# Block 0 of a fused attention and two-MLP kernel: low parts issued before squares, weight conversions issued behind later landmarks

## The chip, the cores and the metric

The kernel runs on one core of a Trainium2 chip. The metric is the device time of one execution in microseconds (us), lower is better. Five engines run at the same time, each working through its own queue in order: PE (matrix multiply), DVE, ACT and POOL (vector work of different kinds), and SP, which here only issues DMA transfers.

## The reference

Attention over 4 batches, 8 heads, 576 positions and 64 channels per head. Four heads see a window of 32 positions back, four see every 32nd position. Its output, 2304 tokens of 512 channels, goes through a gated MLP with a root mean square norm and then through a second MLP without a nonlinearity:

```python
x = attention(q, k, v).transpose(0, 2, 1, 3).reshape(2304, 512)
xn = x / sqrt(mean(x * x) + 1e-6) * rms_g
g = xn @ w_gate;  val = xn @ w_val            # 512 -> 1536
x = (g * sigmoid(g) * val) @ w_out            # 1536 -> 512
out = ((x @ w_a) * (x @ w_b)) @ w_out2        # 512 -> 1536 -> 512
```

All of it is float32. Every large product is made of three matmuls on numbers split into a high part (rounded) and a low part (the rest): high by high, high by low, low by high.

## The kernel before

The 576 positions are cut into six blocks t = 0 to 5 of 96 positions in 4 batches, so 384 tokens each. In block t the loop over fc = 0 to 11 takes 128 of the 1536 hidden channels at a time (a chunk). For each chunk PE makes `g_ps` and `v_ps` (12 matmuls each, lines 478 to 480), DVE scales g by the inverse root (`sg`, line 750), ACT applies Silu (751), DVE multiplies (`h`, 761), ACT rounds h to its high part and POOL or DVE subtracts for the low part (502, 503), and PE adds the chunk into `y` (12 matmuls, the same lines). While block t runs its MLP, the attention of block t + 1 is made in slots between the chunks. Three PSUM tiles serve all `g_ps` and `v_ps`, so `v_ps` of chunk 1 waits for `sg` of chunk 0, and `g_ps` of chunk 2 waits for `h` of chunk 0. The second MLP follows after block 5.

Block 0 has two things more. Its attention has nothing to hide behind: local heads (`qk`, `smask`, `lmax`, `lexp`, `lnorm`, then `pt`, a transpose on PE of the softmax weights, `ptc`, its copy on ACT, and `pv`, the product with v) and strided heads (`sqk`, `sexp`, `snorm`, `spv`). The result is split into `xx` by `xhl`: ACT writes the high part (`xhi`, 384), DVE the low part (`xlo`, 386), and ACT squares (`sq`, 429) for a matmul with ones (433), whose root (`sqrt`, 445) gives `rinv` (447). And block 0 converts the weights of the first MLP, which arrive as 64 bit words, once for all blocks: per 128 x 512 third ACT scales the upper word (134), the lower word is shifted into `cz` (139 on ACT or 136 on DVE, by the table `LOW`), DVE joins both (142), ACT rounds to the high part (147), POOL subtracts (148). `gv` of chunks 1 to 10 is done two thirds at a time (128 x 1024), `wo`, the third for `y`, alone.

The engines' orders are not written by hand. The framework's scheduler lists each engine's instructions by their place in the program and by its own idea of times; `tc.issue_after(i)` (in `gate` and `behind`) puts the instructions of the block behind i in the queue if both are on the same engine, and adds no wait across engines. `GATES` names for each chunk which steps of the attention its conversion stands behind. Two readers of one PSUM tile on different engines are kept apart by the framework: the second one in the program waits for the first.

Of the kernel before, what the change touches and what calls it, by code (L numbers as in the profile page):

```python
# [10 lines left out]
F32 = mybir.dt.float32  # L11
# [4 lines left out]
ALU = mybir.AluOpType  # L16
# [9 lines left out]
NFC = FF // 128  # L26
# [15 lines left out]
          "ptc2 pv0 pvc0 pv1 pvc1 xst0 xst1 xstc0 id36 xstc1 rms rinv")  # L42
WARM = 20

GATES = ["pvm snorm sqr",
         "norm pvm snorm sqr",
         "pvr snorm xhi",
         "snorm sqr sqrt xhi",
         "rec sexp snorm sqrt xhi"]

# [14 lines left out]
WLO = ["PPP", "PPP", "PPP", "PPP", "PPP", "PPP",  # L65
       "PPP", "PPP", "PPP", "PPP", "PPP", "PPD"]

LOW = ["AAA"] * NFC
NEG = -1000000000.0
BIG = 3.0e38  # L70
SCALE = 1.0 / 8.0
# [3 lines left out]
def fused_kernel(ctx: ExitStack, tc: tile.TileContext, qtl, ktl, vl, qs, ks, vs, cst, w1, w2, out):  # L75
# [5 lines left out]
    nc = tc.nc  # L81

    def engine(c):
        return {"P": nc.gpsimd, "D": nc.vector}[c]
# [82 lines left out]
    def run(steps):  # L167
        for f in steps:
            f()
# [14 lines left out]
    def attention(t, pool, psum, banks):  # L184
# [4 lines left out]
        st = {}  # L189
        steps = {}  # L190

        def bank():
            return psum.tile([128, 512], F32, tag=next(banks), name="att")

        def piece(tag, name, bufs):
            return pool.tile([128, NTB], F32, tag=tag, name=name, bufs=bufs)
# [161 lines left out]
        def ptc(g):  # L358
            def f():
                rows, n, keys, units = GROUPS[g]  # L360
                k0 = 0 if g < 2 else 64
                src = st["pps", g][k0:k0 + n].rearrange("k (u h r) -> k u h r", h=2, r=rows // 2)
                for hf in range(2) if g == 2 else [g]:
                    dst = pts[hf][k0:k0 + n, :, :, k0:k0 + rows // 2]
                    nc.scalar.copy(dst, src[:, 4 * hf:4 * hf + 4] if g == 2 else src)
            return f

        def pv(p):
# [11 lines left out]
        def xhl(i, src):  # L380

            xx = act.tile([128, 2, NTB], F32R, tag="x", name="xx", bufs=8)
            hi, lo = xx[:, 0], xx[:, 1]
            st["xhi"] = nc.scalar.activation(hi, src, AF.Copy, scale=g_sb[:, i:i + 1])
            sq(i)()
            st["xlo"] = nc.vector.scalar_tensor_tensor(lo, src, g_sb[:, i:i + 1], hi.bitcast(F32), op0=ALU.mult, op1=ALU.subtract)
            xt[t, i] = xx

        def xsplit(i, src):
# [35 lines left out]
        def sq(i):  # L425
            def f():
                q_t = st["sq", i] = piece("sq", "sq", 2)
                src = st["ops" if i < 2 else "xps", i % 2][:, :NTB]
                nc.scalar.activation(q_t, src, AF.Square)
                if t == 0:  # L430
                    if i == 0:
                        st["rps"] = bank()
                    nc.tensor.matmul(st["rps"][:, :NTB], ones, q_t, start=i == 0, stop=i == 3)
                elif i:
                    engine(SQA[t]).tensor_tensor(q_t, q_t, st["sq", i - 1], op=ALU.add)
            return f
# [50 lines left out]
    def tmp(name):  # L487
        return act.tile([128, NTB], F32, tag="t", name=name, bufs=NTMP)

    made = []  # L490

    @contextmanager
    def behind(instructions):

        with ExitStack() as e:
            for i in instructions:
                e.enter_context(tc.issue_after(i))
            yield
# [17 lines left out]
    g_sb = cst_sb[:, 384:388]  # L516
# [19 lines left out]
    def load_late(which):  # L536
        raw.update(zip(which, load_pair(w1, which, pool)))

    def convert1(fc):
        t = gv[fc] = gv_slot(F32R, "gv")  # L540
        two = [raw.pop((fc, k)) for k in range(2)]
        if fc in FUSEDW:
            both, ready = gvraw[fc], t.rearrange("p k a n -> p (k a) n")
            run(conversion(both.rearrange("p k a n -> p (k a) n"), ready, pool, engine(WLO[fc][0]), LOW[fc][0]))
        else:
            run(zipped(*(conversion(two[k], t[:, k], pool, engine(WLO[fc][k]), LOW[fc][k]) for k in range(2))))

# [29 lines left out]
    @contextmanager  # L577
    def gate(fc):

        with ExitStack() as e:  # L580
            for key in GATES[min(fc, len(GATES) - 1)].split():
                e.enter_context(tc.issue_after(s0["st"][key].ins))
            yield
# [136 lines left out]
    for t in range(NB):  # L720
        if t == 1:
            apool.close()
            pool = apool.enter_context(tc.tile_pool(name="attn", bufs=1))
        if t == NB - 1:
            apool.close()
            cpool.close()
            pool = p2.enter_context(tc.tile_pool(name="forms", bufs=1, reuse_waits="tile"))
            early = [f for k in (4, 5, 0, 1, 2, 3) for f in convert_forms(k, k < 4)]
        nxt = attention(t + 1, pool, psum, itertools.cycle(["att"])) if t + 1 < NB else None
        x = [xt[t, cc] for cc in range(NCC)]  # L730
        for fc in range(NFC):
            if t > 0 and fc == 0:
                load_wo(t, 0)
            g_ps = psum.tile([128, 512], F32, tag="gv", name="g_ps", bufs=3)
            mm_in(g_ps[:, :NTB], gv[fc], 0, x)
            v_ps = psum.tile([128, 512], F32, tag="gv", name="v_ps", bufs=3)
            mm_in(v_ps[:, :NTB], gv[fc], 1, x)
            if t == 0 and fc + 1 < NFC:
                with gate(fc + 1):
                    convert1(fc + 1)  # L740
                if fc + 2 == NFC:
                    load_late([(NFC - 2, 2), (NFC - 1, 2)])
            if t == NB - 1:
                slab[fc] = wgt.tile([128, 4 * DM], F32 if fc in (0, 1, 11) else F32R, tag="gv", name="slab", bufs=NFC)
                with behind(made):
                    run(early[len(early) * fc // NFC:len(early) * (fc + 1) // NFC])
                    for k in [k for k in x0 if k <= fc]:
                        run(x0.pop(k))
            sg = tmp("sg")
            nc.vector.tensor_tensor(sg, g_ps[:, :NTB], ri[t], op=ALU.mult)  # L750
            nc.scalar.activation(sg, sg, AF.Silu)  # L751
            if fc == 1 and t > 0:
                evac_y(t - 1)
            if nxt is not None:
                attention_slot(nxt, fc)
            if prev is not None:
                emit_y(*prev)
            if t > 0 and fc + 1 < NFC:
                load_wo(t, fc + 1)
            h = tmp("h")  # L760
            made[:] = [nc.vector.tensor_tensor(h, sg, v_ps[:, :NTB], op=ALU.mult).ins]  # L761
            hl[t, fc] = split(h, engine(HLO0[fc] if t == 0 else HLO[t]))
            if t == 0:
                wt = wo[0, fc] = wo_tile()
                with gate(fc + 1):
                    run(conversion(raw.pop((fc, 2)), wt, pool, engine(WLO[fc][2]), LOW[fc][2], True))
                nc.sync.dma_start(wod[fc], wt.rearrange("p a n -> p (a n)").bitcast(F32))
                if fc % 2:
                    load_units(1)
                if fc == NFC - 3:  # L770
                    load_late([(NFC - 1, 0), (NFC - 1, 1)])
            prev = (t, fc)
    emit_y(*prev)
    evac_y(NB - 1)
# [238 lines left out]
```

## Time and profile before

| what | value |
|---|---|
| median of 3 runs | 980.23 us (980.2 to 981.69) |
| the profiled execution | 981.02 us |
| its span in the trace | 979.2 us |
| granted TensorE clock, mean | 0.986 |
| PE busy | 949.2 us |
| ACT, POOL, DVE busy | 427.7, 555.1, 620.4 us |

The span runs from the first to the last instruction of the program in the trace. All times in the trace's rows count from the span's start.

### The profile page before, as it was taken

The page shows a single profiled execution, that of the slowest core. Times are in us where ns is not written, and L with a number is a line of the kernel's source. Part 1 is how long each engine was busy: PE and PEld are TensorE (multiplying, and loading weights), DVE is VectorE, ACT ScalarE, POOL GpSimd, SP SyncE. Part 2 cuts the span into 40 slices and gives each one's busy share as a digit, 9 for nine tenths or more (in the row PEclk, how much of TensorE's full clock was granted, in tenths as well). Part 3 has the DMA queues.
Part 4 walks back from the last instruction along what each step waited for, and adds up shares of the span by engine and source line. Part 5 has one row for each costly group of instructions (what it writes and reads, how often), then busy time and mean ns, then how long its engine had stood idle before and what let it go on. Part 6 is the DMA issues. An engine that isn't in the chain of part 4 may idle for free.

```text
span 979.2 us, 14353 instructions
## 1 busy us (share of the span) xinstructions
PE 949.2 (97%) x5438; PEld 900.8 (92%) x5438; DVE 620.4 (63%) x891; ACT 427.7 (44%) x800; POOL 555.1 (57%) x418
## 2 busy tenths in 40 slices
PE   6899999999999999999999899999999999999998
PEld 5799989999999999999999899999999999999996
DVE  5568757638917984988565458667655655465534
ACT  4999645243534423433456455535434423122110
POOL 3489946558739776969468644754743424123211
PEclk7899999999999999999999999999999999999999
DMA  9963375435633643532687975897893973853701
GB/s 339 408 238 119 117 284 206 147 111 178 191 110 126 208 161 107 175 121 80 217 328 278 374 284 209 330 419 312 325 386 122 351 305 117 295 233 150 269 11 65
DMA packets 57364, 215.57 MB, mean 220 GB/s; under 512 B 5968, under 2 KB 14544, under 8 KB 51664
## 3 DMA queue, kind: packets, MB, share of 16 engines
q1 hardware_dynamic: 57296, 214.66, 59.7%
q8 instruction: 43, 0.70, 0.3%
q14 instruction: 25, 0.20, 0.1%
HBM read 172.17 MB, written 42.47 MB: 219 GB/s over the span
## 4 chain that ended last, share of the span: by engine, by line
PE 75%; DVE 6%; DMA 5%; POOL 5%; ACT 4%; issue 3%; SPq 1%; DVEq 0%; POOLq 0%; ACTq 0%
PE o L892 5%; PE o L894 5%; PE o L893 5%; PE Y L838 4%; PE Y L837 4%; PE Y L836 4%; PE y L478 3%; PE g_ps L478 3%; PE v_ps L478 3%; PE g_ps L480 3%; PE v_ps L480 3%; PE g_ps L479 3%; PE v_ps L479 3%; PE y L479 3%; PE y L480 3%
## 5 line engine op out<-in xcount | busy, mean ns | idle before, releaser
L148 POOL TENSOR_TENSOR hl<-c,hl 128x384 fp32r<-128x384 f32 x72 | 77.9, 1082 | 180.5 <-ACT hl L147 173.9
L245 POOL TENSOR_TENSOR prod<-kv_t,qs_t 128x512 f32<-128x512 f32 (+12 forms) x57 | 106.1, 1883 | 18.3 <-DMA kv_t<-in_ks 6.3
L503 POOL TENSOR_TENSOR hl<-h,hl 128x384 fp32r<-128x384 f32 x70 | 77.9, 1113 | 59.7 <-ACT hl L502 59.7
L478 PE MATMUL g_ps<-xx,gv 128*128 128x384 f32 x288 | 98.4, 342 | 5.1 <-DVE h L761 5.0
L478 PE MATMUL v_ps<-xx,gv 128*128 128x384 f32 x288 | 97.5, 339 | 3.5 <-DVE sg L750 3.0
L278 POOL TENSOR_TENSOR prod<-kv_t,S_t 128x512 f32<-128x512 f32 (+12 forms) x57 | 86.0, 1522 | 24.0 <-DVE S_t L270 7.7
L479 PE MATMUL y<-hl,wo 128*128 128x384 f32 x288 | 96.8, 341 | 1.3 <-POOL hl L503 1.3
L479 PE MATMUL v_ps<-xx,gv 128*128 128x384 f32 x288 | 97.8, 340 | 0.0
L480 PE MATMUL g_ps<-xx,gv 128*128 128x384 f32 x288 | 97.5, 339 | 0.0
L479 PE MATMUL g_ps<-xx,gv 128*128 128x384 f32 x288 | 97.3, 339 | 0.0
L480 PE MATMUL v_ps<-xx,gv 128*128 128x384 f32 x288 | 97.2, 338 | 0.0
L843 DVE TENSOR_TENSOR c<-c,Y 128x384 f32<-128x384 f32 x108 | 58.8, 551 | 58.6 <-PE Y L838 53.5
L480 PE MATMUL y<-hl,wo 128*128 128x384 f32 x288 | 95.4, 339 | 0.0
L281 DVE TENSOR_REDUCE xs_t<-prod 128x64 f32<-128x448 f32 (+17 forms) x57 | 85.2, 1515 | 6.0 <-POOL prod L278 5.8
L478 PE MATMUL y<-hl,wo 128*128 128x384 f32 x288 | 83.8, 343 | 2.8 <-DMA wo<-wod 1.8
L892 PE MATMUL o<-slab,hl 128*128 128x512 f32 x216 | 84.7, 393 | 1.0 <-DVE slab L901 0.5
L893 PE MATMUL o<-slab,hl 128*128 128x512 f32 x216 | 84.5, 392 | 0.0
L894 PE MATMUL o<-slab,hl 128*128 128x512 f32 x216 | 83.2, 394 | 0.0
L147 ACT CAST hl<-c 128x384 fp32r<-128x384 f32 x72 | 37.0, 514 | 94.2 <-DVE c L873 93.9
L751 ACT ACTIVATE sg<-sg 128x384 f32<-128x384 f32 x72 | 37.8, 525 | 87.6 <-DVE sg L750 78.0
L838 PE MATMUL Y<-slab,form 128*128 128x384 f32 x216 | 73.0, 338 | 0.0
L837 PE MATMUL Y<-slab,form 128*128 128x384 f32 x216 | 72.9, 338 | 0.0
(135 smaller groups left out, 2521.3 us busy)
## 6 DMA issues: line engine op xcount, KB each, us to landing
form<-formd SPq DMA_DIRECT2D x32, 1792.0 KB, 10.5
wo<-wod SPq DMA_DIRECT2D x60, 512.0 KB, 3.3
raw<-in_w SPq DMA_DIRECT2D x42, 512.0 KB, 7.4
gv_raw<-in_w SPq DMA_DIRECT2D x30, 512.0 KB, 10.0
formd<-form SPq DMA_DIRECT2D x6, 1792.0 KB, 7.0
formd<-forms SPq DMA_DIRECT2D x6, 1792.0 KB, 12.9
slab<-x2d SPq DMA_DIRECT2D x24, 384.0 KB, 4.5
wod<-wo SPq DMA_DIRECT2D x12, 512.0 KB, 3.4
```

The lines of the kernel that those rows point to most:

```text
L148: lo_eng.tensor_tensor(lo, x, hi.bitcast(F32), op=ALU.subtract)
L245: nc.gpsimd.tensor_tensor(pr, st["ks", g][:, :, :n, :], st["qs"][:, heads(g), mm:mm + 1, :].to_broadcast([128, G, n, D]), op=ALU.mult)
L278: st["pvm"] = nc.gpsimd.tensor_tensor(pr, st["vs", g][:, :, :n, :], st["S"][:, heads(g), mm, :n, None].to_broadcast([128, G, n, D]), op=AL ...
L281: st["pvr"] = nc.vector.tensor_reduce(st["xs"][:, mm, heads(g), :], pr.rearrange("p g n d -> p g d n"), axis=X, op=ALU.add)
L478: nc.tensor.matmul(out_ps, w_hi, x_hi, start=start, stop=False)
L479: nc.tensor.matmul(out_ps, w_hi, x_lo, start=False, stop=False)
L480: nc.tensor.matmul(out_ps, w_lo, x_hi, start=False, stop=stop)
L837: nc.tensor.matmul(bank(n), hi, x[p][:, 1, c], start=False, stop=False, skip_group_check=not begins)
L838: nc.tensor.matmul(bank(n), lo, x[p][:, 0, c], start=False, stop=c == 1, skip_group_check=not begins)
L892: nc.tensor.matmul(o, h[:, 0, cols], w[0], start=n == 0, stop=False)
L893: nc.tensor.matmul(o, h[:, 0, cols], w[1], start=False, stop=False)
L894: nc.tensor.matmul(o, h[:, 1, cols], w[0], start=False, stop=n == len(chunks) - 1)
```

## The change

Four edits, all for block 0: (1) in `xhl` the low part stands ahead of the square in the program; (2) `GATES` for chunks 0 and 1 add the copies of the transposed local weights (`ptc1`, `ptc2`), and chunk 2 now stands behind `sqr`, `sqrt` and `xhi`; `wo` of chunk 0 takes the gate of chunk 2; (3) the lower words of `gv` 1 and 2 are shifted on DVE instead of ACT; (4) the conversions of `gv` of chunk fc + 1 and of `wo` of chunk fc stand behind the three instructions that make `h` and its parts of chunk fc - 3.

```diff
-GATES = ["pvm snorm sqr",
-         "norm pvm snorm sqr",
-         "pvr snorm xhi",
+GATES = ["pvm snorm sqr ptc1",
+         "norm pvm snorm sqr ptc2",
+         "snorm sqr sqrt xhi",
          "snorm sqr sqrt xhi",
          "rec sexp snorm sqrt xhi"]
...
-LOW = ["AAA"] * NFC
+LOW = ["AAA", "DDA", "DDA"] + ["AAA"] * 9
...
-                    nc.scalar.copy(dst, src[:, 4 * hf:4 * hf + 4] if g == 2 else src)
+                    st[f"ptc{g}"] = nc.scalar.copy(dst, src[:, 4 * hf:4 * hf + 4] if g == 2 else src)
...
             st["xhi"] = nc.scalar.activation(hi, src, AF.Copy, scale=g_sb[:, i:i + 1])
+            st["xlo"] = nc.vector.scalar_tensor_tensor(lo, src, g_sb[:, i:i + 1], hi.bitcast(F32), op0=ALU.mult, op1=ALU.subtract)
             sq(i)()
-            st["xlo"] = nc.vector.scalar_tensor_tensor(lo, src, g_sb[:, i:i + 1], hi.bitcast(F32), op0=ALU.mult, op1=ALU.subtract)
...
+    h_made = {}
...
-                with gate(fc + 1):
+                with gate(fc + 1), behind(h_made.get(fc - 3, [])):
                     convert1(fc + 1)
...
-                with gate(fc + 1):
+                with gate(max(fc + 1, 2)), behind(h_made.get(fc - 3, [])):
                     run(conversion(raw.pop((fc, 2)), wt, pool, engine(WLO[fc][2]), LOW[fc][2], True))
...
+            if t == 0:
+                h_made[fc] = list(made)
```

On PE, ACT, DVE, POOL and SP the order changes from the first softmax to about the third chunk of block 1; behind that it is the same. Three places follow. The lines of the changed kernel are one higher from line 490 on, and one lower for `xlo` (385).

DVE from the sum of the last local softmax group (341, 343, 344, 345 normalise it) to the inverse root; `prod` is the product of the strided heads, `xx` the split result. Before:

```order
L341 TENSOR_REDUCE lsm<-s_t 64x8
L270 TENSOR_TENSOR S_t<-S_t,srs 128x12x3
L142 SCALAR_TENSOR_TENSOR cz<-gv_raw,cz 128x512
L343 TENSOR_SCALAR lsm<-lsm 64x8
L142 SCALAR_TENSOR_TENSOR cz<-gv_raw,cz 128x512
L344 RECIPROCAL lrs<-lsm 64x8
L281 TENSOR_REDUCE xs_t<-prod 128x256
L345 TENSOR_TENSOR s_t<-s_t,lrs 64x512
...
L386 SCALAR_TENSOR_TENSOR xx<-att,cst_sb,xx 128x384 x2
L142 SCALAR_TENSOR_TENSOR cz<-gv_raw,cz 128x1024
L142 SCALAR_TENSOR_TENSOR cz<-gv_raw,cz 128x512
L386 SCALAR_TENSOR_TENSOR xx<-att,cst_sb,xx 128x384 x2
```

And of the change:

```order
L341 TENSOR_REDUCE lsm<-s_t 64x8
L269 RECIPROCAL srs<-ssm 128x12
L343 TENSOR_SCALAR lsm<-lsm 64x8
L270 TENSOR_TENSOR S_t<-S_t,srs 128x12x3
L344 RECIPROCAL lrs<-lsm 64x8
L345 TENSOR_TENSOR s_t<-s_t,lrs 64x512
...
L136 TENSOR_SCALAR cz<-gv_raw 128x1024
L142 SCALAR_TENSOR_TENSOR cz<-gv_raw,cz 128x1024
L385 SCALAR_TENSOR_TENSOR xx<-att,cst_sb,xx 128x384
L136 TENSOR_SCALAR cz<-gv_raw 128x1024
L385 SCALAR_TENSOR_TENSOR xx<-att,cst_sb,xx 128x384 x3
```

Two joins (142) and a reduce no longer stand ahead of the normalisation 345, and two joins no longer stand ahead of the last two low parts; two shifts (136) are new.

ACT from the root of block 0 (445) to the first Silu (the activation into `sg`). Before:

```order
L445 ACTIVATE rms_t<-att,eps_sb 128x384
L134 ACTIVATE gv_raw<-gv_raw 128x1024
L139 ACTIVATE cz<-gv_raw 128x1024
L134 ACTIVATE gv_raw<-gv_raw 128x512
L134 ACTIVATE gv_raw<-gv_raw 128x1024
L139 ACTIVATE cz<-gv_raw 128x1024
L134 ACTIVATE gv_raw<-gv_raw 128x512 x2
L139 ACTIVATE cz<-gv_raw 128x512
L134 ACTIVATE gv_raw<-gv_raw 128x512
L134 ACTIVATE gv_raw<-gv_raw 128x1024
L147 CAST gv<-cz 128x2x512
L751 ACT_TABLE_LOAD
```

And of the change:

```order
L445 ACTIVATE rms_t<-att,eps_sb 128x384
L134 ACTIVATE gv_raw<-gv_raw 128x512
L139 ACTIVATE cz<-gv_raw 128x512
L134 ACTIVATE gv_raw<-gv_raw 128x1024
L134 ACTIVATE gv_raw<-gv_raw 128x512
L134 ACTIVATE gv_raw<-gv_raw 128x1024
L139 ACTIVATE cz<-gv_raw 128x1024
L134 ACTIVATE gv_raw<-gv_raw 128x512
L147 CAST wo<-cz 128x512
L147 CAST gv<-cz 128x2x512
L752 ACT_TABLE_LOAD
```

Eleven instructions stood between root and Silu's table, nine stand there now, other ones: behind the root there is now the whole conversion of `gv` 2 and of `wo` 0, which used to be done ahead of it.

DVE at the change from block 0 to block 1, where `S_t` are the strided scores of block 2 (their `prod` comes from POOL), `ys` is the output of block 0, `sg` and `h` belong to chunks of block 1. Before:

```order
L761 TENSOR_TENSOR h<-sg,v_ps 128x384
L248 TENSOR_REDUCE S_t<-prod 128x7
L248 TENSOR_REDUCE S_t<-prod 128x8
L750 TENSOR_TENSOR sg<-g_ps,rinv 128x384
L604 TENSOR_TENSOR ys<-y_537,rinv 128x384
...
L248 TENSOR_REDUCE S_t<-prod 128x9
L311 SCALAR_TENSOR_TENSOR s_t<-att,cst_sb 128x384
L248 TENSOR_REDUCE S_t<-prod 128x7
L320 TENSOR_REDUCE lmx<-s_t 128x4
L761 TENSOR_TENSOR h<-sg,v_ps 128x384
```

And of the change:

```order
L762 TENSOR_TENSOR h<-sg,v_ps 128x384
L751 TENSOR_TENSOR sg<-g_ps,rinv 128x384
L248 TENSOR_REDUCE S_t<-prod 128x7
L605 TENSOR_TENSOR ys<-y_537,rinv 128x384
...
L248 TENSOR_REDUCE S_t<-prod 128x9
L762 TENSOR_TENSOR h<-sg,v_ps 128x384
L311 SCALAR_TENSOR_TENSOR s_t<-att,cst_sb 128x384
```

The `sg` of block 1's second chunk now stands ahead of the reduces that wait for POOL, and its `h` ahead of the mask (311), one reduce and the maximum (320).

## Rows read from the trace of the kernel before

**Rows 1.** The page's head: span; busy time, share and instructions by engine.

```profile
span 979.2 us, 14353 instructions
PE 949.2 (97%) x5438; PEld 900.8 (92%) x5438; DVE 620.4 (63%) x891; ACT 427.7 (44%) x800; POOL 555.1 (57%) x418
```

**Rows 2.** Busy us (x instructions) of PE, PEld, DVE, ACT, POOL; granted clock, DMA, GB/s.

```profile
75.00:100.00 25.00, 23.95 (x162) 22.92 (x162) 22.20 (x26) 23.36 (x45) 25.00 (x14) 1.00 0.34 117
100.00:125.00 25.00, 24.34 (x147) 22.36 (x146) 17.57 (x21) 16.34 (x32) 22.15 (x17) 1.00 0.40 146
...
200.00:225.00 25.00, 25.00 (x149) 24.67 (x148) 12.75 (x18) 10.06 (x17) 14.85 (x12) 1.00 0.30 95
```

**Rows 3.** Timeline, 18 to 39 us: start, duration, engine, line, operation, tiles.

```profile
18.96 0.68 DVE L341 TENSOR_REDUCE lsm<-s_t 64x8 f32<-64x512 f32 x1 [0.86 <-ACT s_t L330]
...
22.70 0.67 DVE L345 TENSOR_TENSOR s_t<-s_t,lrs 64x512 f32<-64x512 f32 x1
...
25.93 0.64 ACT L365 COPY pt<-att 64x256 f32<-64x256 f32 x2
...
26.40 2.83 PE L375 MATMUL att<-pt,v_t 128*64 128x96 f32 x32
...
32.00 0.62 DVE L386 SCALAR_TENSOR_TENSOR xx<-att,cst_sb,xx 128x384 fp32r<-128x384 f32 x1 [1.45 <-ACT sq L429]
...
35.00 1.82 DVE L142 SCALAR_TENSOR_TENSOR cz<-gv_raw,cz 128x1024 uint32<-128x1024 uint32 x2 [2.38 <-ACT cz L139]
...
35.21 0.42 PE L478 MATMUL g_ps<-xx,gv 128*128 128x384 f32 x1
...
36.75 1.14 DVE L386 SCALAR_TENSOR_TENSOR xx<-att,cst_sb,xx 128x384 fp32r<-128x384 f32 x2
...
37.72 1.45 PE L433 MATMUL att<-sq,ones 128*128 128x384 f32 x4
```

**Rows 4.** Timeline of ACT and DVE, 39 to 51 us.

```profile
39.21 0.58 ACT L445 ACTIVATE rms_t<-att,eps_sb 128x384 f32<-128x384 f32 x1 [0.90 <-PE att L433]
39.69 1.16 ACT L134 ACTIVATE gv_raw<-gv_raw 128x1024 f32<-128x1024 f32 x1
39.83 2.55 DVE L447 RECIPROCAL rinv<-rms_t 128x384 f32<-128x384 f32 x1 [1.95 <-ACT rms_t L445]
...
40.71 1.15 ACT L139 ACTIVATE cz<-gv_raw 128x1024 uint32<-128x1024 uint16 x1
...
48.61 1.28 ACT L751 ACT_TABLE_LOAD   x1
49.90 0.52 ACT L751 ACTIVATE sg<-sg 128x384 f32<-128x384 f32 x1
```

**Rows 5.** ACT groups by form, 14 to 60 us: count, busy us, mean ns.

```profile
L134 ACT ACTIVATE gv_raw<-gv_raw 128x512 f32<-128x512 f32 x10 | 6.5, 677 | 0.0
```

**Rows 6.** Timeline of PE at its longest wait in block 0.

```profile
51.07 0.69 PE L478 MATMUL g_ps<-xx,gv 128*128 128x384 f32 x1 [4.71 <-DVE h L761]
```

**Rows 7.** Windows with a lower granted clock; columns as in rows 2.

```profile
50.60:53.90 3.30, 2.83 (x9) 2.83 (x10) 0.88 (x2) 3.30 (x5) 2.87 (x3) 0.50 1.07 405
...
153.00:156.30 3.30, 3.30 (x12) 3.30 (x11) 2.08 (x5) 3.27 (x11) 2.52 (x4) 0.50 0.37 103
```

**Rows 8.** DVE groups by form, 14 to 60 us.

```profile
L142 DVE SCALAR_TENSOR_TENSOR cz<-gv_raw,cz 128x1024 uint32<-128x1024 uint32 x6 | 7.3, 1215 | 5.8 <-ACT cz L139 5.8
```

**Rows 9.** POOL groups by form, 20 to 130 us; behind the bar idle us, releasers.

```profile
L148 POOL TENSOR_TENSOR gv<-cz,gv 128x1024 fp32r<-128x1024 f32 x10 | 26.8, 2685 | 14.5 <-ACT gv L147 12.2 <-DMA gv_raw<-in_w 2.3
```

**Rows 10.** Timeline, end of block 0.

```profile
116.77 0.69 ACT L134 ACTIVATE raw<-raw 128x512 f32<-128x512 f32 x1 [2.10 <-DMA raw<-in_w]
...
144.36 0.44 PE L478 MATMUL v_ps<-xx,gv 128*128 128x384 f32 x1 [1.04 <-DVE sg L750]
...
151.73 0.54 DVE L761 TENSOR_TENSOR h<-sg,v_ps 128x384 f32<-128x384 f32 x1
...
152.32 0.44 PE L478 MATMUL g_ps<-xx,gv 128*128 128x384 f32 x1 [0.31 <-DVE h L761]
```

## Prediction

> **What bounds the kernel now.** The page's head comes first: PE is busy for 949.2 of 979.2 us [rows 1], so all else counts only where PE waits. The table by stretches of 25 us, read next, says where that is. From 200 us on PE is busy without a gap at full clock, with DVE, ACT and POOL at 41 to 60% [rows 2]: a microsecond gained or lost before that moves the end by as much. Between 75 and 125 us PE is nearly full as well, but so are its suppliers: ACT 23.36 of 25 us, POOL 25.00 of 25, then 16.34 and 22.15 [rows 2]. What is left is the time to 51 us and the step from block 0 to block 1.
>
> The timeline of the front, read as a chain: the last softmax group is summed on DVE at 18.96 but normalised only at 22.70, because joins of weights that wait for ACT stand between. So the copies of its transpose come at 25.93, the product with v at 26.40, and the first real matmul, `g_ps`, at 35.21 [rows 3]. The first low parts wait for squares (1.45 us on ACT), the last two for joins, and end at 37.89, after `g_ps` has begun; the squares' matmuls come late too, and the root starts at 39.21 [rows 3, 4]. Then ACT works through eleven conversion instructions before it loads Silu's table at 48.61; the first Silu starts at 49.90 [rows 4]. `h` of chunk 0 needs it, `g_ps` of chunk 2 needs the PSUM tile that `h` frees, and PE waits 4.71 us for it, until 51.07 [rows 6]. Behind that wait the granted clock is 0.50, the lower of the two levels, 1.2 GHz, for 3.3 us [rows 7].
>
> **The change, part by part.** I start all chains from rows that the new order leaves in place and go on in the new order.
>
> *Softmax to first matmul.* The sum 341 ends at 19.64 as before. Now 269, 343, 270 and 344 follow, small operations of some 0.2 us, and 345 starts at about 20.5 and ends at 21.2 instead of 23.37: 2.2 us earlier. Before, its end stood 2.56 us ahead of the copies (25.93); with the same distance they start at 23.75. ACT has the second copy and four scalings and shifts of 128 x 512 ahead of them, from 20.3 on, 0.57 and 4 times 0.55, ready at 23.1, so it does not hold them. A 512 column step on ACT is 0.55 because 128 x 1024 steps are 1.02 from start to start for a duration of 1.15 [rows 4], and 0.68 [rows 5] less the same 0.13 is 0.55. The product with v, its 2.83 us and the warming matmuls up to `g_ps` are the same instructions as before (only the squares' matmuls move among them), so `g_ps` starts 2.2 earlier, at 33.0.
>
> *Low parts.* Their new place costs nothing and is worth little by itself: on DVE they end at about 31.8 instead of 37.89, so that all twelve matmuls of `g_ps` run in one piece. The two shifts on DVE are not in the trace. The nearest row is the join of 128 x 1024, 1.22 [rows 8], with two inputs where the shift has one; the lower end is half of it, 0.6, the upper 1.82, what two joins took together at 35.00 [rows 3]. I take 1.1, near the one join. With 1.82 twice the last low part would end at 33.2, and it is first read by the eleventh matmul, at 34.7: nothing at either end. What they spare ACT (1.01 each) is in the next sums.
>
> *Root.* The squares' last two matmuls stand now behind 12 and 18 real matmuls. 18 at 0.17 (149 in 25 us [rows 2]) are 3.1, two squares' matmuls 1.45 [rows 3]: 33.0 + 3.1 + 1.45 = 37.6 instead of 39.21. A loss hides here: ACT has its squares done at 32.3 and waits for the root until 37.6, some 5.3 us in which it used to convert. Everything queued behind the root on ACT (conversions of `gv` 2 on, `wo` 0 on) pays for it later.
>
> *Root to Silu.* Now nine instructions: three scalings and one shift of 512 (4 x 0.55), two scalings and one shift of 1024 (3 x 1.02), a cast of 512 (0.55) and one of 1024 (1.0): 6.8. With 0.48 for the root's step and 1.29 for the table's, 8.57 instead of 10.69 [rows 4]. Silu starts at 46.2, 3.7 earlier, and `h` frees PE's tile at 47.4 instead of 51.07: **-3.7 us**.
>
> *Next wait.* In `g_ps` of chunk 2 the new order puts matmuls of `y` that need the high part of `h` 0; ACT has a cast (1.0) and a shift (0.55) ahead of it, so it ends at 48.75, and PE, with four matmuls to do (0.7), waits 0.65: **+0.7**.
>
> *Clock.* PE waits twice, about 2.5 us for `sg` 0 and 2.1 us for `h` 0. I take one stretch at the lower clock as before: 0. If it is gone, 3.3 us at half speed become 1.65 us of work: -1.7. The Trainium skill, TensorE: Matmul & The Clock Gate, section HAM oscillation, says that idle gaps under a certain length leave the clock alone, which by itself would give the -1.7. The trace agrees on the 4.71 us wait and not at the other place: the clock also fell at 153 us, behind waits of 1.04 and 0.31 us [rows 7, 10].
>
> *Chunks 3 to 10.* The four-ahead rule puts `h` and Silu ahead of conversions that nobody needs yet. POOL's list in the new order, at 2.4 a `gv` (2.69 with disturbances [rows 9]), ends each low part 0 to 10 us before PE, running 3.3 us earlier than now, asks for it. I take 0, with -0 and +3 as bounds (below).
>
> *Step to block 1.* `sg` of its second chunk no longer stands behind reduces that wait for POOL, which ends PE's 1.04 us wait at 144.36; `h` at 151.73, for which PE waits until 152.32 [rows 10], stands three instructions earlier. I take **-1.2** for the first and 0 for the second; both, with the lower clock behind them, would be -3.
>
> Sum: -3.7 + 0.7 - 1.2 = -4.2. On the profiled execution's 981.0 us (span 979.2 and 1.8 around it) that is 976.8; that execution lay 0.8 above the median, so the runs should show **976.0 us**, -0.43%.
>
> **The rivals.**
>
> *Larger gain, the clock.* If two waits of 2 to 2.5 us with matmuls between them leave the clock at 2.4 GHz, and the softer step to block 1 does too, 1.7 us comes back twice: 976.0 - 3.4 = 972.6. For it: no wait would be as long as 4.71. Against it: the fall at 153 us.
>
> *No change, the late loads.* The thirds of chunk 11 and the last `wo` come through two buffers, each load waiting for a conversion; ACT stood 2.10 us for one at 116.77 [rows 10]. Those conversions stand in POOL's and ACT's queues behind work that the new order brings forward. If the first of them is no earlier than now, PE runs into it 3 us sooner and waits 3 us longer; only the -1.2 is left: 979.0. For it: POOL is full from 75 to 100 us. Against: POOL has waited 12.2 us for ACT's casts [rows 9], so it can start earlier.
>
> *Slower, ACT's lost wait.* When Silu 0 starts, the new order has three 512 scalings, two 512 shifts, one 512 cast, one scaling, one shift and one cast of 1024 fewer behind it: 6 x 0.55 + 3.0 = 6.3 us, while it is 3.7 ahead, so 2.6 us behind in work. ACT has 1.64 us idle in 75 to 100 us and 8.66 in the next 25 [rows 2]. If PE's need falls before that slack, block 0 goes at ACT's pace: the 4.2 gained is lost, 2.6 added, and a further fall of the clock (1.7) with it: 980.2 + 4.3 = 984.5. It decides where a `gv` high part ends later than about 3 us ahead of its first matmul.
>
> *The edits don't bind* is no rival: the order shows them on every engine.
>
> **How the numbers follow.** A change of this kernel is told from none at about 0.2%, 2 us. Forecast (974 to 978) 0.50; larger gain 0.16; late loads 0.19; ACT's lost wait 0.15. Faster: 0.50 + 0.16 = 0.66; the late loads are the 0.19 within 0.2%; slower 0.15. The range leaves out the slow case and the far end of the large gain: 971.8 to 981.5; the likeliest case's own is 974 to 978.
>
> **What would show it.** Right: the copies at about 23.8, `g_ps` from about 33.0, the root at 37.6, Silu at 46.2, `g_ps` of chunk 2 at 47.4, no 1 us wait for `sg` in block 1, and the lead on PE kept through chunk 11. Wrong in the front: PE's first matmuls held by POOL's low parts or by squares. Wrong in the middle: PE waits of over 1 us with ACT `gv` or POOL `gv` as releaser between 55 and 110 us (slow rival), or a longer wait for the thirds of chunk 11 near 115 to 120 us (late loads). Wrong in the clock: lower-clock windows fewer or more than two between 35 and 160 us.

## The result, and the profile after

The changed kernel takes **986.33 us** (median of 4, 985.16 to 986.9) beside 980.22 for the kernel before: ratio 1.0058 (95% interval 1.0046 to 1.007), slower by some 6 us. The forecast was faster, 976.0; the range ended at 981.5.

The page's head after, to be read beside [rows 1]:

```profile
span 984.5 us, 14361 instructions
PE 951.4 (97%) x5438; PEld 901.9 (92%) x5438; DVE 627.0 (64%) x893; ACT 425.0 (43%) x798; POOL 552.4 (56%) x418
```

PE is busy for 2.2 us more with the same matmuls, and waits for the rest. The front does what was predicted. Timeline of the changed kernel, copies to `g_ps` of chunk 2 (start, duration, engine, line, operation, tiles, idle time before):

```profile
23.12 0.64 ACT L365 COPY pt<-att 64x256 f32<-64x256 f32 x2
...
26.29 1.75 DVE L136 TENSOR_SCALAR cz<-gv_raw 128x1024 uint32<-128x1024 uint32 x1 [0.41 <-POOL gv L148]
...
29.81 0.68 DVE L136 TENSOR_SCALAR cz<-gv_raw 128x1024 uint32<-128x1024 uint32 x1
...
33.41 0.42 PE L478 MATMUL g_ps<-xx,gv 128*128 128x384 f32 x1
...
37.29 0.81 PE L433 MATMUL att<-sq,ones 128*128 128x384 f32 x2
...
38.13 0.58 ACT L445 ACTIVATE rms_t<-att,eps_sb 128x384 f32<-128x384 f32 x1 [4.39 <-PE att L433]
...
46.79 0.52 ACT L752 ACTIVATE sg<-sg 128x384 f32<-128x384 f32 x1
...
47.96 0.45 PE L478 MATMUL g_ps<-xx,gv 128*128 128x384 f32 x1 [0.55 <-DVE h L762]
```

`g_ps` of chunk 2 starts 3.1 us earlier than in [rows 6]. But ACT stands still for 4.39 us ahead of the root, where [rows 4] have 0.90: the last matmul of the squares stands on PE behind 18 real ones, and everything that ACT used to convert meanwhile is gated behind the root. ACT's groups from 19 to 39 us, the kernel before (behind the bar busy us, mean ns, then idle time before and its releaser):

```profile
L134 ACT ACTIVATE gv_raw<-gv_raw 128x512 f32<-128x512 f32 (+1 forms) x5 | 4.3, 865 | 0.0
L139 ACT ACTIVATE cz<-gv_raw 128x512 uint32<-128x512 uint16 (+1 forms) x5 | 4.3, 859 | 0.0
L147 ACT CAST gv<-cz 128x512 fp32r<-128x512 f32 (+1 forms) x4 | 3.3, 844 | 0.3 <-DVE cz L142 0.3
...
L147 ACT CAST wo<-cz 128x512 fp32r<-128x512 f32 x2 | 1.3, 645 | 1.1 <-DVE cz L142 1.1
```

The same, the changed kernel:

```profile
L134 ACT ACTIVATE gv_raw<-gv_raw 128x512 f32<-128x512 f32 (+1 forms) x4 | 3.1, 784 | 0.0
L147 ACT CAST gv<-cz 128x512 fp32r<-128x512 f32 (+1 forms) x3 | 2.3, 761 | 2.3 <-DVE cz L142 2.3
...
L139 ACT ACTIVATE cz<-gv_raw 128x512 uint32<-128x512 uint16 x2 | 1.3, 658 | 0.0
...
L445 ACT ACTIVATE rms_t<-att,eps_sb 128x384 f32<-128x384 f32 x1 | 0.6, 582 | 4.4 <-PE att L433 4.4
```

16 conversion instructions (13.2 us) stand against 9 (6.7 us). Counted from the program's start to 39 us, those that have ended are 18 (14.6 us) and 8 (6.1 us), and only some 2 us of the difference went to DVE with the two shifts. PE's next long wait comes 45 us later, the others from 118 us on. Timeline of the changed kernel, where PE, and ACT ahead of it, wait:

```profile
79.30 1.28 ACT L333 ACT_TABLE_LOAD   x1
...
84.67 0.52 ACT L752 ACTIVATE sg<-sg 128x384 f32<-128x384 f32 x1
...
86.31 0.69 PE L478 MATMUL g_ps<-xx,gv 128*128 128x384 f32 x1 [4.06 <-DVE h L762]
...
119.71 0.96 PE L480 MATMUL y<-hl,wo 128*128 128x384 f32 x4 [1.11 <-POOL wo L148]
...
121.51 0.33 SPq L108 DMA_DIRECT2D raw<-in_w  x1
...
122.10 1.50 PE L441 MATMUL att<-sq,ones 128*128 128x384 f32 x2 [1.43 <-DVE sq L435]
...
125.19 0.68 ACT L134 ACTIVATE raw<-raw 128x512 f32<-128x512 f32 x1 [0.57 <-DMA raw<-in_w]
...
128.06 0.44 PE L478 MATMUL g_ps<-xx,gv 128*128 128x384 f32 x1 [1.36 <-ACT gv L147]
...
130.91 0.67 ACT L134 ACTIVATE raw<-raw 128x512 f32<-128x512 f32 x1 [2.31 <-DMA raw<-in_w]
...
134.61 0.44 PE L478 MATMUL v_ps<-xx,gv 128*128 128x384 f32 x1 [1.87 <-ACT gv L147]
```

Until about 82 us the lead of the front is kept: `g_ps` of chunk 6 starts at 77.12, before at 81.43. It is lost in the two stretches behind. From 82 to 112 us and from 112 to 140, before and then after (columns as in [rows 2]):

```profile
82.00:112.00 30.00, 28.95 (x199) 27.45 (x198) 25.70 (x29) 23.99 (x38) 30.00 (x20) 1.00 0.30 109
112.00:140.00 28.00, 26.81 (x146) 24.68 (x146) 16.41 (x22) 17.69 (x31) 14.71 (x12) 1.00 0.65 225
```

```profile
82.00:112.00 30.00, 25.70 (x165) 24.11 (x164) 23.88 (x30) 26.18 (x48) 24.37 (x17) 0.89 0.24 84
112.00:140.00 28.00, 22.22 (x105) 20.09 (x104) 15.43 (x17) 17.99 (x32) 17.41 (x14) 0.88 0.45 164
```

PE is idle for 4.3 and 5.8 us there, where it was for 1.1 and 1.2, and part of its work runs at the lower clock. The first third of chunk 11 is asked for at 121.51, nine us later than before (112.43), and ACT starts on it at 125.19 where [rows 10] have 116.77. `g_ps` of chunk 11 goes from 119.80 to 128.06. Stretches of the changed kernel with a lower clock (columns as in [rows 2]):

```profile
43.80:47.10 3.30, 3.30 (x12) 3.23 (x11) 0.92 (x1) 3.27 (x5) 2.49 (x2) 0.50 1.07 413
84.80:91.40 6.60, 5.09 (x16) 5.09 (x17) 6.13 (x9) 6.60 (x10) 2.02 (x2) 0.50 0.22 60
122.30:125.60 3.30, 3.30 (x9) 2.69 (x9) 1.47 (x2) 2.52 (x4) 2.58 (x3) 0.50 0.70 248
135.90:139.20 3.30, 3.30 (x13) 3.30 (x12) 0.20 (x1) 2.25 (x4) 1.31 (x2) 0.50 0.04 15
```

16.5 us at 1.2 GHz, where [rows 7] show 6.6. The account of PE from its first `g_ps` to the `g_ps` of block 1's fourth chunk, before and then after (length, busy us, clock, DMA share, GB/s):

```profile
35.21:152.32 117.11, 106.71 (x643) 0.99 0.60 221
```

```profile
33.41:157.99 124.58, 111.48 (x636) 0.93 0.58 210
```

The stretch is 7.5 us longer: 2.7 us of it is more idle time (13.1 against 10.4), 4.8 us is more busy time, much of the same work being done at the lower clock. It starts 1.8 us earlier, so 5.7 us are lost at its end, and 5.3 of them are left at the end of the span.

### The profile page after: what moved, and what is told of

Same layout as the page of the kernel before. It is cut to its first block, busy times and chain, and to the rows that moved or that the text cites. A ratio compares the mean times of both kernels' runs of the same rounds, so it can differ in the third digit from the quotient of the medians.

```text
span 984.5 us, 14361 instructions
## 1 busy us (share of the span) xinstructions
PE 951.4 (97%) x5438; PEld 901.9 (92%) x5438; DVE 627.0 (64%) x893; ACT 425.0 (43%) x798; POOL 552.4 (56%) x418
## 4 chain that ended last, share of the span: by engine, by line
PE 68%; DMA 9%; DVE 8%; POOL 6%; ACT 5%; issue 3%; SPq 1%; DVEq 0%; POOLq 0%; ACTq 0%
PE o L895 5%; PE o L897 5%; PE o L896 5%; PE Y L841 4%; PE Y L840 4%; PE Y L839 4%; DMA gv_raw<-in_w 3%; PE y L478 3%; PE v_ps L478 3%; PE v_ps L480 3%; PE v_ps L479 3%; PE y L479 3%; PE y L480 3%; PE g_ps L478 3%; PE g_ps L480 3%
## 5 line engine op out<-in xcount | busy, mean ns | idle before, releaser
L478 PE MATMUL v_ps<-xx,gv 128*128 128x384 f32 x288 | 99.2, 345 | 5.2 <-DVE sg L751 3.3
L479 PE MATMUL v_ps<-xx,gv 128*128 128x384 f32 x288 | 98.8, 343 | 0.0
L479 PE MATMUL y<-hl,wo 128*128 128x384 f32 x288 | 98.2, 341 | 0.4 <-POOL hl L504 0.3
L480 PE MATMUL v_ps<-xx,gv 128*128 128x384 f32 x288 | 98.2, 341 | 0.0
L480 PE MATMUL y<-hl,wo 128*128 128x384 f32 x288 | 93.1, 337 | 1.1 <-POOL wo L148 1.1
L478 PE MATMUL y<-hl,wo 128*128 128x384 f32 x288 | 87.5, 347 | 2.4 <-DMA wo<-wod 1.9
```

The source lines that it names most:

```text
L478: nc.tensor.matmul(out_ps, w_hi, x_hi, start=start, stop=False)
L479: nc.tensor.matmul(out_ps, w_hi, x_lo, start=False, stop=False)
L480: nc.tensor.matmul(out_ps, w_lo, x_hi, start=False, stop=stop)
```

## The experiments

The first theory after the result was not ACT's lost wait but the late `wo`: nine us late at the end, all `wo` conversions 9 to 13 us late, so the four-ahead rule and `wo`'s gate would be the cause. Edits are numbered as in the change: 1 low parts, 2 gates, 3 shifts, 4 the rule. Each time is the median of 4 to 12 executions, in us, with the interval of its ratio to the kernel before. Where a run's ratio is given as us, it is taken of 980.7, about the median of the kernel before beside each run (980.69 to 980.99). Rows and starts are those of one profiled execution of each run.

**The halves of the change.**

E1, edits 1 to 3 alone:

```diff
-                with gate(fc + 1), behind(h_made.get(fc - 3, [])):   # gv
+                with gate(fc + 1):
-                with gate(max(fc + 1, 2)), behind(h_made.get(fc - 3, [])):   # wo
+                with gate(fc + 1):
```

> The three edits of the front alone; the two conversions of each chunk have the old gates and no four-ahead rule. If the late conversions of wo are what cost (they run 9 to 13 us later in the changed kernel, and the loads into the two raw buffers, the last chunk's gv and its matmuls follow them), they come about 3 us earlier than before here, the lead of 3.3 to 3.8 us of PE at chunks 2 and 3 is kept through chunk 11, and the time is 976 to 977.5. If it is ACT's lost wait before the root (work held back by the front's gates), the conversions are late without the rule too: first matmul of chunk 11 at 122 to 128 us, time 983 to 986.

E2, edit 4 alone: the kernel before with these two lines as changed.

> The fourth edit alone on the kernel before: the four-ahead rule on both conversions and the later gate of wo 0. If the late wo conversions cost, they are late here without any lead at the front: last chunk's gv 8 to 10 us later than before, time 986 to 989. If ACT's lost wait is the cause, the front is the old one and nothing is lost: 979 to 981.

E3, the changed kernel with both `behind(...)` taken out, `gate(max(fc + 1, 2))` kept; E4, with the one on `wo` taken out.

> The changed kernel without the four-ahead rule on either conversion; the later gate of wo 0 stays. If the rule makes the wo conversions late: last chunk at its old time less 3 us, 976 to 978. If the gate alone pushes them back (wo 0 ends at 45.9 instead of 28.9 us): still 8 us late at chunk 11, 983 to 986. If ACT's lost wait: 983 to 986 too, told from the gate by the kernel with the front's edits alone.

> The changed kernel with the four-ahead rule taken off the wo conversions only. If it is the rule on wo: 976 to 979, with wo 8 converted by about 117 us as before and the chunk 11 thirds asked for by about 112. If it is the rule on gv that delays the last chunk: no change from the changed kernel, 985 to 987.

Measured: E1 **989.9** (1.0081 to 1.0107), E2 **982.1** (1.0001 to 1.0022), E3 **991.2** (1.0094 to 1.0131), E4 **989.7** (1.0073 to 1.0099). The rule's part in this theory falls at once: without the rule the kernel is slower, not faster. The rule gives back 3.5 us of the 9.2 that the front costs, and on the kernel before it brings `g_ps` of chunk 2 from 51.07 to 48.19. Every kernel with the changed front shows ACT idle for over 4.3 us ahead of the root. E1 and E3 lie above what I had for ACT's lost wait too (986 at most), E4 above both of its cases, and E2 a little above its better one.

**The entries of the front.** From the changed kernel: E5 undoes chunk 2's gate, E6 all three gates, E7 the first two, E8 the shifts.

```diff
-         "snorm sqr sqrt xhi",                            # E5, E6: chunk 2
+         "pvr snorm xhi",
-GATES = ["pvm snorm sqr ptc1", "norm pvm snorm sqr ptc2",   # E6, E7
+GATES = ["pvm snorm sqr", "norm pvm snorm sqr",
-LOW = ["AAA", "DDA", "DDA"] + ["AAA"] * 9               # E8
+LOW = ["AAA"] * NFC
```

> The changed kernel with one entry undone: the conversions of gv 2, wo 0 and wo 1 stand again behind chunk 2's old gate (behind the third row of transposes, not behind the root). The runs so far speak for ACT's lost wait: the changed kernel leaves ACT idle for 4.39 and 0.71 us ahead of the root, 33 to 38 us, and all that it held back there is late by chunk 11. By that, ACT is idle for under 1.5 us there, gv 2 is cast before 43 us instead of 45.48, PE keeps 3 us of lead through chunk 11 and the time is 975 to 978. If it is the four-ahead rule that makes wo late, nothing comes back: 985 to 987.

> The changed kernel with all three gates as before; low parts ahead of squares, shifts on DVE and the four-ahead rule stay. By ACT's lost wait: no long idle time on ACT ahead of the root, first real matmul about 1 to 2 us later than in the changed kernel (the copies of transposed weights go behind conversions again), time 976 to 979. If the rule is the cause: 985 to 988.

> The changed kernel with the gates of the first two conversions as before, and chunk 2's gate as changed: the counterpart of the kernel with only chunk 2's gate undone. By ACT's lost wait through chunk 2's gate: first real matmul back at about 35 us and the loss stays, 986 to 989. If it is the copies standing ahead of the first conversions that cost: 979 to 982.

> The changed kernel with the shifts of chunks 1 and 2 on ACT again, as before the change. By ACT's lost wait, ACT gets 3 to 4 us more to do, part of it in the time ahead of the root where it was idle: within 2 us of the changed kernel, 985 to 988. If DVE's shift (1.75 us beside POOL, at 26.29) and what it holds up are the cause: 981 to 984.

Measured: E5 **983.9** (1.0023 to 1.0051), E6 **983.5** (1.0014 to 1.0035), E7 **986.25** (1.0043 to 1.0067), E8 **989.6** (1.0079 to 1.0113). Chunk 2's gate matters and the first two don't, as expected of ACT's lost wait; two shifts more for ACT cost 3.7 us more. But E5 and E6, for which I had 975 to 979 by ACT's lost wait, stay some 3 us above the kernel before with ACT idle for only 1.00 and 1.25 us ahead of the root. The root itself is late there, 41.31 and 42.29 instead of 39.21: in the order the last squares stand behind conversions. That points to edit 1, the one that I had priced at nothing.

**Single edits on the kernel before.** E9 changes chunk 2's gate alone, E10 swaps low part and square alone, E11 is the rule alone with `gate(fc + 1)` kept for `wo`, E12 is E11 with the changed `LOW`.

```diff
-         "pvr snorm xhi",                # E9
+         "snorm sqr sqrt xhi",
+            st["xlo"] = nc.vector.scalar_tensor_tensor(...)    # E10
             sq(i)()
-            st["xlo"] = nc.vector.scalar_tensor_tensor(...)
-                with gate(fc + 1):      # E11, E12: gv and wo
+                with gate(fc + 1), behind(h_made.get(fc - 3, [])):
```

> The kernel before with one entry changed: chunk 2's gate (gv 2, wo 1) behind the root and the first squares, nothing else. ACT's lost wait: ACT has 14.6 us of conversion instructions (scalings, shifts, casts) done by 39 us in the kernel before and 6.1 in the changed one, of which two shifts of about 1.1 went to DVE. If the gate is what makes the difference, this kernel has under 10 us done by 39, over 3 us of idle ACT ahead of the root, and 984 to 989. If the gate costs only together with the other edits: 980 to 982.

> The kernel before with the low parts ahead of the squares, nothing else. I priced it at nothing. If that holds: 979.5 to 981.5. The order shows two conversions and a cast of ACT ahead of the last square now; if that counts, the root starts 1 to 2 us later than 39.21 and the time is 982 to 984.

> The four-ahead rule alone on the kernel before, with the old gate for wo 0 too. The rule with the later wo gate gained 2.9 us at chunk 2 and gave 982.1: if the wo gate eats the gain (2.3 us less conversion on ACT by 33 us), 977 to 979.5; if the rule itself does (wo 3 to wo 8 some 3 us later), 981 to 983.

> The kernel before with the four-ahead rule and the two shifts of chunks 1 and 2 on DVE; all gates and the place of the low parts as before. If ACT's conversion work in the first 105 us sets the end of block 0, the 2.2 us that the shifts take from ACT come back (the changed kernel lost 3.3 us when they went back to ACT): 976 to 979, faster than both kernels. If it is the order behind chunk 2 alone: within 1 us of the kernel with the rule alone.

Measured: E9 **990.1** (1.008 to 1.0106), E10 **990.5** (1.0087 to 1.0116), E11 **977.75** (0.9957 to 0.998), E12 **979.5** (0.998 to 0.9997). Each of the two front edits costs more alone than the whole change, and more than I had expected (989 and 984 at most). Timeline of E9, ACT at the root, the first Silu, and PE behind it:

```profile
37.92 0.58 ACT L445 ACTIVATE rms_t<-att,eps_sb 128x384 f32<-128x384 f32 x1 [3.92 <-PE att L433]
...
50.19 0.52 ACT L751 ACTIVATE sg<-sg 128x384 f32<-128x384 f32 x1
...
51.35 0.69 PE L478 MATMUL g_ps<-xx,gv 128*128 128x384 f32 x1 [6.29 <-DVE h L761]
```

The root is 1.3 us earlier than in [rows 4], Silu is not. And of E10, where the gates are the old ones:

```profile
34.45 0.88 ACT L429 ACTIVATE sq<-att 128x384 f32<-128x384 f32 x2
...
37.08 0.49 ACT L429 ACTIVATE sq<-att 128x384 f32<-128x384 f32 x1 [0.30 <-PE att L433]
...
40.30 0.81 PE L433 MATMUL att<-sq,ones 128*128 128x384 f32 x2
...
41.15 0.58 ACT L445 ACTIVATE rms_t<-att,eps_sb 128x384 f32<-128x384 f32 x1 [3.58 <-PE att L433]
...
54.61 0.69 PE L478 MATMUL g_ps<-xx,gv 128*128 128x384 f32 x1 [4.49 <-DVE h L761]
```

This is the mechanism of edit 1. A square now stands behind its low part, and ACT's queue has four conversion instructions ahead of the second square (before: ahead of the third) and two casts ahead of the fourth, which ends at 37.57. PE meanwhile is among its real matmuls: 36 of them stand ahead of the last square's matmul, at 40.30, where 14 stood before. The root is 1.9 us late, ACT idles for 3.58 us, and `g_ps` of chunk 2 is 3.5 us late. E11 is the version that beats both kernels: root at 39.69 after 1.06 us of idle time, Silu's end at 46.85, `g_ps` of chunk 2 at 47.49 and of chunk 11 at 119.05. E2 differs from E11 only in the later gate of `wo` and is 4.2 us slower, so that half of the first theory does cost, on the kernel before. E12 lies 1.9 us above E11, outside both ranges that I had: DVE's shifts, worth 3.7 us inside the change (E8), cost rather than gain there. Why was not tried.

**Idle time or order?** E13 is the changed kernel and E14 the kernel before, both with chunk 2 gated behind the last square (ACT's own instruction) and not behind the root; E15 is E13, and E16 the changed kernel, with the old gate for `wo`.

```diff
-                nc.scalar.activation(q_t, src, AF.Square)
+                st["sqd"] = nc.scalar.activation(q_t, src, AF.Square)
...
+         "snorm sqr sqd xhi",                 # chunk 2, E13 to E15
...
-                with gate(max(fc + 1, 2)), behind(h_made.get(fc - 3, [])):   # E15, E16
+                with gate(fc + 1), behind(h_made.get(fc - 3, [])):
```

> The changed kernel with chunk 2's gate behind the last square on ACT instead of behind the root; all else as changed. ACT can convert while it waits for the root, and the squares stay ahead. If the idle time costs: ACT idle for under 2 us ahead of the root instead of 5.1, over 10 us of conversion done by 39 us instead of 6.1, 977 to 981. If it is the new order behind the root or the rule: 984 to 987.

> The kernel before with chunk 2's gate behind the last square (squares first, then conversions, then the root). The gate behind the root cost 9.3 us here. If that was the idle time: 979 to 983. If any shift of chunk 2's conversions behind the squares costs as much: 987 to 991.

> The changed kernel with chunk 2's gate behind the last square and wo 0's gate as before. wo 0 goes back into the time ahead of the root (some 2.3 us of ACT). The same step gained 4.4 us in the kernel with the rule alone. If ACT's conversion work done by the root is what counts: 1 to 4 us faster than with the later wo gate, 974 to 978; otherwise the same within 1 us.

> The changed kernel with wo 0's gate as before, chunk 2's gate still behind the root. By ACT's lost wait: 2 to 3 us come back, 983 to 984.5; the 4 us of idle time ahead of the root stay. If the wo gate mattered only for the kernel with the rule alone: 985.5 to 987.

Measured: E13 **983.9** (1.0019 to 1.004), E14 **983.7** (1.001 to 1.0032), E15 **981.1** (0.9997 to 1.0014), E16 **987.1** (1.0052 to 1.0076). The first three gain less than idle time alone was to give (981, 983 and 978 at most). Timeline of E14, ACT from the last square to the root:

```profile
33.17 0.49 ACT L429 ACTIVATE sq<-att 128x384 f32<-128x384 f32 x1 [0.55 <-PE att L433]
33.56 1.14 ACT L134 ACTIVATE gv_raw<-gv_raw 128x1024 f32<-128x1024 f32 x1
...
37.00 1.05 ACT L147 CAST gv<-cz 128x1024 fp32r<-128x1024 f32 x1 [0.16 <-DVE cz L142]
37.95 0.58 ACT L445 ACTIVATE rms_t<-att,eps_sb 128x384 f32<-128x384 f32 x1
```

The root starts when it did in E9 (37.95 and 37.92); ACT converts in the 4 us ahead of it instead of standing still. That is worth 7 us: +9.1 us in E9, +2.1 in E14. In the changed kernel it gives back 2.7 us (E13), with the old `wo` gate 5.2 (E15). With ACT idle at the root the old `wo` gate gives nothing (E16): there it puts conversions ahead of the squares, and the root slips to 41.29. E9 and E14 also differ in the order behind the root, so the 7 us is the idle time and what it does to that order. E14 has no idle time at the root, and an earlier root, and is still 2.1 us slower than the kernel before: that rest is the later place of chunk 2's conversions, by a way that stays open.

The wait at 86 us is not simply the price of the idle time. E2, whose front is the old one and whose ACT is busy for 11.96 us from 25 to 39 us (before 12.64, changed 7.11), has the same wait behind the same exponentials and table loads. ACT's first load, the Silu behind the second, and PE in E2:

```profile
77.50 1.28 ACT L333 ACT_TABLE_LOAD   x1
...
83.42 0.52 ACT L752 ACTIVATE sg<-sg 128x384 f32<-128x384 f32 x1
...
84.59 0.44 PE L478 MATMUL g_ps<-xx,gv 128*128 128x384 f32 x1 [3.14 <-DVE h L762]
```

And E13, which fills the idle time, waits 3.92 us for an `h` at 83.01, where the changed kernel waits 4.06 at 86.31.

**The price of the low parts inside the change.** E17 is E11 with the first two gates and the shifts as changed, E18 is E17 with edit 1; E18 with the later `wo` gate is E5.

```diff
+            st["xlo"] = nc.vector.scalar_tensor_tensor(...)    # E18 over E17
             sq(i)()
-            st["xlo"] = nc.vector.scalar_tensor_tensor(...)
```

> The four-ahead rule, the first two gates and the shifts on DVE as changed; chunk 2's gate, wo 0's gate and the place of the low parts as before. ACT should have 12 to 13 us of conversion done by 39 us (14.6 in the kernel before less 2.2 of shifts) and wait under 2 us for the root. By ACT's lost wait: 976 to 979.5, faster than before. If the first gates cost by themselves: 981 to 983.

> The kernel of the run beside it, with the low parts ahead of the squares. The order puts conversions ahead of the last two squares on ACT, so their matmuls should stand behind more real ones on PE, and the root start 1.5 us later or more with ACT idle for over 3 us ahead of it: 3 to 6 us slower than the run beside it. If the low parts' place costs only without the other edits: within 1 us of it.

Measured: E17 **980.9** (0.9991 to 1.0012), E18 **985.6** (1.0038 to 1.0062). The roots of E17, then E18:

```profile
39.35 0.58 ACT L445 ACTIVATE rms_t<-att,eps_sb 128x384 f32<-128x384 f32 x1 [1.93 <-PE att L433]
```

```profile
40.78 0.58 ACT L445 ACTIVATE rms_t<-att,eps_sb 128x384 f32<-128x384 f32 x1 [2.95 <-PE att L433]
```

E17 lies above what I had by ACT's lost wait (979.5 at most), E18 is 4.8 us slower than it, as expected (3 to 6). So a chain of single steps leads to the changed kernel. The kernels on it stand, in us against the kernel before (each with about 1.2 us to either side), at -3.1 (E11, the rule), -1.2 (E12, shifts), +0.1 (E17, first gates), +4.9 (E18, low parts), +3.6 (E5, later `wo` gate) and +5.7 (the changed kernel, chunk 2's gate). The steps are thus -3.1, +1.9, +1.3, **+4.8**, -1.3 and **+2.1**: in this order the low parts are the largest loss, and the two steps of 1.3 are hardly clear of the noise. The table puts the runs side by side: us against before, the root's start, ACT's idle time just ahead of it, ACT busy in the 14 us from 25 to 39, `g_ps` of chunk 2, of chunk 11, of block 1's fourth chunk, and us at 1.2 GHz between 35 and 160.

| kernel | us | root | idle | ACT | chunk 2 | chunk 11 | block 1 | 1.2 GHz |
|---|---|---|---|---|---|---|---|---|
| E11 | -3.1 | 39.69 | 1.06 | 12.64 | 47.49 | 119.05 | 151.54 | 6.8 |
| before | 0 | 39.21 | 0.90 | 12.64 | 51.07 | 119.80 | 152.32 | 6.8 |
| E15 | +0.5 | 38.95 | 0.58 | 10.79 | 47.32 | 128.21 | 153.06 | 13.7 |
| E14 | +2.1 | 37.95 | 0 | 12.91 | 50.37 | 122.50 | 155.42 | 10.2 |
| E13 | +2.9 | 37.55 | 0 | 11.27 | 45.36 | 127.13 | 154.12 | 10.2 |
| E18 | +4.9 | 40.78 | 2.95 | 10.16 | 49.54 | 127.86 | 157.53 | 13.7 |
| changed | +5.7 | 38.13 | 4.39 | 7.11 | 47.96 | 128.06 | 157.99 | 17.1 |
| E9 | +9.1 | 37.92 | 3.92 | 9.21 | 51.35 | 132.84 | 161.45 | 20.5 |
| E1 | +9.2 | 38.34 | 4.45 | 7.07 | 51.35 | 132.63 | 160.56 | 13.7 |
| E10 | +10.0 | 41.15 | 3.58 | 11.54 | 54.61 | 136.74 | 163.92 | 23.9 |

An early `g_ps` of chunk 2 tells nothing of the end. Idle time of ACT at the root does: where it is about 3 us or more, the kernel in this table loses 5 to 10 us. The other runs fit: E3, E4, E7, E8 and E16 (4.3 to 4.8 us idle) lose 5.4 to 11.1, while E2, E5, E6, E12 and E17 (under 2) stand between -1.2 and +3.6, the late roots of E5 and E6 at +3.6 and +2.5.

## Why the prediction was wrong

*Softmax to first matmul*: right. Copies at 23.12 (predicted 23.75), `g_ps` at 33.41 (33.0).

*Low parts*: the first step that failed, "their new place costs nothing". The end was right (32.48 against 31.8), and so was the sum of the two shifts, 1.75 + 0.68 against twice 1.1. What I left out is the other side of the swap: where the low part goes first, the square goes second, and on ACT's queue conversions fill the place between. Inside the change it costs 4.8 us (E18 against E17), alone 10.0 (E10).

*Root* and *Root to Silu*: right in time, 38.13 (37.6) and 46.79 (46.2). The sentence "ACT has its squares done at 32.3 and waits for the root until 37.6" named the loss, with 5.3 us; measured are 4.39 and, ahead of the last square, 0.71.

*Next wait*: right in kind. `g_ps` of chunk 2 stands at 47.96 (47.4), after a wait of 0.55 us, and PE's wait for the high part of `h` 0 behind it is 0.23 us where I had 0.65.

*Chunks 3 to 10*: the step that turned the forecast round, "I take 0", with 3 us at the far end. The lost wait of the step before was not carried into it, except as a rival. Filling the same idle time is worth 7 us on the kernel before (E9 against E14) and 2.7 in the changed one (E13). I compared POOL's list with PE's need; but POOL waits for ACT's casts, and ACT had no time to make up the loss: from 39 to 105 us it is busy for 62.8 of 66 in the changed kernel and 61.7 in the kernel before, so by these sums the debt runs on to chunk 11. This road is argued, not shown: with the idle time filled, chunk 11 starts only 0.9 us earlier (E13, 127.13), and with two shifts less on ACT E12 is slower than E11. Shown is what the two edits cost.

*Clock*: predicted 0. Four stretches at the lower clock stand where two did before, and PE's busy time carries 4.8 of the 7.5 us that its stretch grew by, more than the 2.7 us of added idle time. I had also read the fall at 153 us as standing behind waits of 1.04 and 0.31 us and overlooked a longer one between them, in the kernel before:

```profile
150.88 1.13 PE L293 MATMUL att<-k_t,q_t 128*128 128x96 f32 x8 [1.14 <-DVE s_t L311]
```

*Step to block 1*: right in kind, too small. From block 1's first `g_ps` (135.07) to that of its fourth chunk (157.99) are 22.92 us, against 25.57 before: -2.65 where I had -1.2. PE was idle for 2.50 us of it before and is not idle at all after: besides the 1.04 and 0.31 us that I had in view, the 1.14 us are gone. The fall of the clock at 153 us, gone too, lay behind this stretch. E11, which has the rule alone and comes there 1.2 us later than the kernel before, takes 23.55.

*The rivals*: "Slower, ACT's lost wait" (0.15) had the direction and one of the two causes. That its time is near (984.5 for 986.3) is in part luck, since its sum has no term for the low parts, 4.8 us. Its sign, PE held by `gv` between 55 and 110 us, was wrong, since PE waited for an `h` at 86.31 (Silu behind the exponentials of the softmax and two table loads, 79.30 to 84.67) and then from 118 us on. "The late loads" are seen too (121.51 instead of 112.43), but as a symptom: the rule alone with the later `wo` gate (E2) has them as well, `g_ps` of chunk 11 at 126.01, and ends 1 us above the kernel before. Open is how much of the wait at 86 us belongs to the order of exponentials and Silu itself: E2 and E13 have it with 3.14 and 3.92 us, E11 has none for an `h` there (it waits 1.49 us until 83.73, for POOL); it wasn't tried apart. A third `raw` buffer wasn't tried either.

*What bounds the kernel*: "without a gap at full clock" from 200 us on was too strong. From 500 to 600 us PE was busy for 96.15 of 100 us, at a mean granted clock of 0.98.

## What to carry to other kernels

The idle time of an engine is not free if that engine is the one that is short later: before a gate is moved, add up the work that it takes out of the wait, and follow the debt to the first place where that engine has slack, here some 65 us on. Swapping two instructions on different engines moves the second one's place in its own queue too; look at what slips in between. A lead won at the front can be lost again at the next place where another engine is behind, here at 86 us. Where a step forward and a step back come in one change, try each alone: here the rule by itself, with the old gate of `wo`, is 3 us faster than before, and two edits of the front cost 9 and 10 us alone.

## What the hardware showed besides

The clock fell behind short waits. Ahead of the fall at 122.3 us PE had waited 1.11 us (until 119.71, for `wo`) and 1.43 us (until 122.10); no wait near it was longer. By the Trainium skill, TensorE: Matmul & The Clock Gate, section HAM oscillation, only idle gaps longer than these are to be avoided; taken as a limit on each single gap, that rule would not have this stretch. The trace has it, as it has the one at 153 us in [rows 7], and it decides. Nor does one such wait always bring a fall: E11 waits 1.49 us until 83.73 and 1.45 until 98.69, and its granted clock stays at 1.00 until 119.4.

The same shift on DVE took 1.75 us at 26.29 and 0.68 at 29.81. Beside the first POOL was subtracting, to 27.48; beside the second it did nothing. POOL in the changed kernel:

```profile
24.98 2.50 POOL L148 TENSOR_TENSOR gv<-cz,gv 128x512 fp32r<-128x512 f32 x2 [1.28 <-ACT gv L147]
```

In the twelve other traces with these shifts the first takes 1.36 to 1.76, with POOL beside it, and the second 0.68 or 0.69, without. The Trainium skill, SBUF — State Buffer, section Who interferes with whom, has DVE and GpSimd share one pair of ports as an exclusive lock. The traces agree: in all thirteen the first shift ends 0.55 or 0.56 us behind the end of the subtraction that POOL had begun before it.
